# Strassen's seven half products for both MLP products after a hashed attention, in float32

## The chip, the cores and the metric

The kernel runs on 1 core of one Trainium2 chip. The time is the device time of one execution in microseconds (us), with the kernel before and the changed kernel run in turn on the same chip. Every time below is a median, with the least and the greatest run beside it.

A word used throughout: the attention works in 32 **units**. Two heads make a pair, there are 16 pairs, and each pair has two units of 384 queries. A unit took some 11.8 us in the kernel before. Even units transpose the next pair's Q and K, odd units compute its hash bits.

## The reference

```python
# attention: q, k, v are (4, 8, 768, 64), proj is (64, 6)
q_bits = (einsum('bhsd,dk->bhsk', q, proj) > 0);  k_bits = (same with k)
mask   = bucket(q_bits) == bucket(k_bits)            # 6 bits equal
scores = where(mask, q @ k.T / sqrt(64), -1e9)
attn   = softmax(scores);  out = attn @ v
# bridge: (4, 8, 768, 64) -> x of (3072, 512)
# MLP: w_in (512, 2048), w_out (2048, 512), alpha (2048,)
h = x @ w_in
g = maximum(h, 0) + alpha * minimum(h, 0)
return g @ w_out
```

## The kernel before

Attention and MLP follow each other. While the attention runs, each unit also decodes one piece of a weight (128 x 512, 512 KB, so 64-bit numbers, turned into float32) on VectorE. TensorE's work of a unit is split so that it always has something to do; the loads for the next pair are issued at the end of a unit. This is the part that the argument touches:

```python
    def load(pi, name, queue=None):
        ...
            t = pool.tile([P, NC, 2, D], F32, name=f"{name}n{pi}", tag=f"{name}n", bufs=1)   # one buffer
            for s in range(2):
                queue.dma_start(t[:, :, s], src[b, 2 * hp + s].rearrange("(p c) d -> p c d", c=NC))
...
    for u in range(UNITS):                        # 32
        pi, g = divmod(u, NCH)
        scores(u, 0)
        ...
        weight_parts(u)                           # VectorE: one weight piece
        scores(u, 1)
        add_third(u)                              # GpSimd: part of the row sums
        weight_sum(u)
        if more:
            if g == 0:
                turn(pi + 1, "k", 0)              # TensorE transposes of K for the next pair
                turn(pi + 1, "k", 1)
            else:
                hash_bits(pi + 1, 1)
        ...
        load_weight(u + 3)
        ...
        if more:
            magnitude(pi + 1, "qk"[g])            # ScalarE: squares of Q (even) or K (odd), in place
            if pi + 2 < NPAIR:
                load(pi + 2, "qk"[g])             # then the buffer is free for the next Q or K
```

So K has a single buffer; its last reader runs at the end of an odd unit, the next load is issued then, and the transposes that need it come in the middle of the following even unit.

The MLP holds both weights in SBUF and is matmuls alone, per half batch:

```python
            for kk in range(NK):                  # 4 k-tiles, 384 columns
                do(PE.matmul(ps, w[:, kk, o : o + P], xT[b][:, kk, ch * CW : (ch + 1) * CW], ...))
...
            for f in range(NF):                   # 16 f-tiles, 512 columns
                do(PE.matmul(ps, gT[b, ch, f][:, t * P : (t + 1) * P], w_out[f // 4][:, f % 4], ...))
```

Of the kernel before, what the change touches and what calls it, by code (L numbers as in the profile page):

```python
# [8 lines left out]
F32 = mybir.dt.float32  # L9
BF16 = mybir.dt.bfloat16  # L10
U32 = mybir.dt.uint32
# [336 lines left out]
@with_exitstack  # L348
def kernel(
    ctx: ExitStack,  # L350
    tc: tile.TileContext,
    q: bass.AP,
    k: bass.AP,
    v: bass.AP,
    proj: bass.AP,
    moe_w_in: bass.AP,
    moe_w_out: bass.AP,
    moe_alpha: bass.AP,
    out: bass.AP,
):  # L360
























    args = (tc, q, k, v, proj, moe_w_in, moe_w_out, moe_alpha, out)
    keep = ctx.enter_context(tc.tile_pool(name="keep", bufs=1))
    flag = keep.tile([1, 1], mybir.dt.int32, name="flag")
    fast_path(*args, flag)
    again = tc.nc.values_load(flag[0:1, 0:1])
    with tc.If(again > 0):  # L390
        general_path(*args)
# [3 lines left out]
def fast_path(  # L395
# [27 lines left out]
    BIG = 2.0 ** 20  # L423
# [9 lines left out]
    first = ctx.enter_context(tc.tile_pool(name="first", bufs=2))  # L433
# [13 lines left out]
    bq = const.tile([P, 1], F32, name="bq")  # L447
    tk = const.tile([P, 1], F32, name="tk")
    mk = const.tile([P, 1], F32, name="mk")
# [5 lines left out]
    w_in = [const.tile([P, NK, DFF // 4], F32, name=f"w_in{i}") for i in range(4)]  # L455
    w_out = [const.tile([P, NF // 4, DM], F32, name=f"w_out{i}") for i in range(4)]
    NW = 4 * (len(w_in) + len(w_out))
    wmax = const.tile([P, NW], F32, name="wmax")
    xT = [const.tile([P, NP, S], F32, name=f"xT{b}") for b in range(B)]

    NPT = 9
# [19 lines left out]
    def setup():  # L481

        for s in range(2):
            do(DVE.memset(wh[s], 0.0))
            nc.sync.dma_start(wh[s][D * s : D * s + D, :NB], proj)
        nc.sync.dma_start(alpha16, moe_alpha.rearrange("(t p) -> t p", p=P))
        make_identity(nc, ident)
        do(DVE.memset(ones, 1.0))
        for s in range(2):
            r = slice(D * s, D * s + D)  # L490
            do(DVE.tensor_copy(wh[s][r, NB : 2 * NB], wh[s][r, :NB]))



        for t, vals, step in (
            (bq, (-1e-37, -1e-37, 1.0, 1.0), 32),
            (tk, (0.0, -3.0e38, -3.0e38, -3.0e38), D),
            (mk, (BIG, -BIG / 2, -BIG / 2 * NB, 0.0), D),
        ):
            do(DVE.memset(t, vals[3]))  # L500
            for r in range(0, P, step):
                do(DVE.memset(t[r : r + 2 * NB + 1], vals[2]))
                do(DVE.memset(t[r : r + 2 * NB], vals[1]))
                do(DVE.memset(t[r : r + NB], vals[0]))
        for t in pts:
            do(POOL.memset(t[:, :, CW : CW + 1], 1.0))
        for t in qbs:
            do(POOL.memset(t, 0.0))
# [7 lines left out]
    raw, wr = {}, {}  # L516

    def piece(i):
        tiles, src = (w_in, moe_w_in) if i < NW // 2 else (w_out, moe_w_out)
        j, o = divmod(i % (NW // 2), 4)  # L520
        if src is moe_w_in:
            w = DFF // 4
            return tiles[j][:, o], src[o * P : (o + 1) * P, j * w : (j + 1) * w]
        return tiles[j][:, o], src[(4 * j + o) * P : (4 * j + o + 1) * P]

    def load_weight(i):
        if i < NW:
            raw[i] = pool.tile([P, 512], moe_w_in.dtype, name=f"raw{i}", tag="raw", bufs=3)
            nc.sync.dma_start(raw[i], piece(i)[1])
# [8 lines left out]
    def weight_abs(i):  # L538
        lo, hi = halves(i)
        do(ACT.activation(piece(i)[0], hi.bitcast(F32), AF.Abs))  # L540

    def weight_parts(i):
        lo, hi = halves(i)
        x = piece(i)[0]
        wr[i] = r = pool.tile([P, 512], F32, name=f"wr{i}", tag="wr")
# [7 lines left out]
    def weight_sum(i):  # L553
        lo, hi = halves(i)
        do(DVE.tensor_tensor(wr[i], piece(i)[0], wr[i], op=ALU.add))
        do(DVE.scalar_tensor_tensor(
            piece(i)[0].bitcast(U32), hi, 0x80000000, wr[i].bitcast(U32), op0=ALU.bitwise_and, op1=ALU.bitwise_or,
        ))


    def turn(pi, name, half):
# [6 lines left out]
        do(ACT.copy(tr[name, pi][:, half * CW : (half + 1) * CW], ps))  # L568
# [7 lines left out]
    def hash_bits(pi, half):  # L576
# [11 lines left out]
        for s in range(2):  # L588
            r = slice(D * s + 32, D * s + D)
            do(ACT.activation(bits["q", pi][D * s : D * s + 32, cols], ps[r], AF.Sign, bias=bq[r]))  # L590
        do(DVE.tensor_scalar(bits["k", pi][:, cols], ps, tk, mk, op0=ALU.is_gt, op1=ALU.mult))  # L591


    def scores(u, part):
        pi, g = divmod(u, NCH)
        qs = slice(g * CW, (g + 1) * CW)
        for kc in (2 * part, 2 * part + 1):
# [10 lines left out]
            do(ACT.activation(pt[:, :, :CW], sc[:, :, :CW], AF.Exp, scale=SCALE))  # L608
# [41 lines left out]
    def divide(u):  # L650
# [11 lines left out]
        do(DVE.scalar_tensor_tensor(  # L662
            xT[b][:, hp, g * CW : (g + 1) * CW], av[u][:, :CW], vsum[pi], d, op0=ALU.add, op1=ALU.mult,
        ))
# [19 lines left out]
    for u in range(UNITS):  # L684
# [17 lines left out]
        weight_sum(u)  # L702
        if more:
            if g == 0:
                turn(pi + 1, "k", 0)
# [3 lines that stand above are left out]
# [8 lines left out]
        load_weight(u + 3)  # L717
        if u + 1 < NW:
            weight_abs(u + 1)
# [6 lines left out]
    gT = {}  # L726

    def ff1(b, ch, f):

        if f % 4 < 2:  # L730
            ps = psum.tile([P, 2, 512], F32, name=f"h{b}_{ch}_{f}", tag="sc")[:, 0, :CW]
        else:
            ps = psum.tile([P, CW], F32, name=f"h{b}_{ch}_{f}", tag="mi")
        w, o = w_in[f // (NF // 4)], (f % (NF // 4)) * P
        for kk in range(NK):
            do(PE.matmul(  # L736
                ps, w[:, kk, o : o + P], xT[b][:, kk, ch * CW : (ch + 1) * CW],
                start=(kk == 0), stop=(kk == NK - 1),
            ))
        early = b == ch == 0 and f < EARLY  # L740
        neg = first.tile([P, CW], F32, name=f"neg{b}_{ch}_{f}", tag="neg")
        do(DVE.tensor_scalar(neg, ps, 0.0, alpha[:, f : f + 1], op0=ALU.min, op1=ALU.mult))  # L742
        where, bufs = (first, EARLY) if early else (mpool[0], NF + 2)
        g = where.tile([P, CW], F32, name=f"g{b}_{ch}_{f}", tag="g", bufs=bufs)
        do(DVE.scalar_tensor_tensor(g, ps, 0.0, neg, op0=ALU.max, op1=ALU.add))  # L745
        gT[b, ch, f] = g

    def ff2(b, ch, t):
        ps = psum.tile([P, DM], F32, name=f"z{b}_{ch}_{t}", tag="av")
        for f in range(NF):  # L750
            do(PE.matmul(  # L751
                ps, gT[b, ch, f][:, t * P : (t + 1) * P], w_out[f // 4][:, f % 4],
                start=(f == 0), stop=(f == NF - 1),
            ))
        o = mpool[0].tile([P, DM], F32, name=f"o{b}_{ch}_{t}", tag="o")
        do(ACT.copy(o, ps))  # L756
        nc.sync.dma_start(out_v[b, ch * CH + t], o)


    def verdict():  # L760
        top = const.tile([P, 3], F32, name="top")
        row = const.tile([1, 3], F32, name="row")
        do(DVE.tensor_reduce(top[:, :2], mags, axis=mybir.AxisListType.X, op=ALU.max))
        do(DVE.tensor_reduce(top[:, 2:3], wmax, axis=mybir.AxisListType.X, op=ALU.max))
        for n in range(3):
            ps = psum.tile([1, P], F32, name=f"vd{n}", tag="mi")
            do(PE.transpose(ps, top[:, n : n + 1], ident))
            do(DVE.tensor_reduce(row[:, n : n + 1], ps, axis=mybir.AxisListType.X, op=ALU.max))
        do(DVE.tensor_tensor(row[:, 0:1], row[:, 0:1], row[:, 1:2], op=ALU.mult))

        do(DVE.tensor_scalar(row[:, 0:1], row[:, 0:1], SAFE, None, op0=ALU.is_le))
        do(DVE.tensor_scalar(row[:, 2:3], row[:, 2:3], HI_END, None, op0=ALU.is_lt))
        do(DVE.tensor_tensor(row[:, 0:1], row[:, 0:1], row[:, 2:3], op=ALU.mult))
        do(DVE.tensor_scalar(flag, row[:, 0:1], -1.0, 1.0, op0=ALU.mult, op1=ALU.add))


    EARLY = 2
    mpool = []
    chunks = [(b, ch) for b in range(B) for ch in range(NCH)]
    last = UNITS - 1  # L780
    attend(last, 0)
    ff1(0, 0, 0)
    add_last(last)
    attend(last, 1)
    ff1(0, 0, 1)
# [3 lines left out]
    mpool.append(ctx.enter_context(tc.tile_pool(name="mlp", bufs=2)))  # L789
    for n, (b, ch) in enumerate(chunks):  # L790
        for f in range(EARLY, NF):
            ff1(b, ch, f)
        if n == 0:
            verdict()
        if n + 1 < len(chunks):
            for f in range(EARLY):
                ff1(*chunks[n + 1], f)
        for t in range(CH):
            ff2(b, ch, t)
# [29 lines left out]
```

## Time and profile before

| | kernel before |
|---|---|
| time | 1066.0 us (1065.7 to 1066.4) |
| span of the profiled execution | 1064.9 us |
| TensorE, VectorE busy in the span | 98%, 47% |
| mean granted clock of TensorE (1 is full speed) | 0.995 |
| attention, MLP | about 395 us, about 670 us |

In the profiles PE is TensorE's matmuls, PEld its weight loads, DVE VectorE, ACT ScalarE, POOL GpSimd and SPq SyncE's queue; L567 is line 567 of the kernel. The profile is read in this order: which engine is busy, then in which stretch of time, then what the idle time of that engine waited for. The chain of waits is the work that ended last, followed back step by step to what released it (start, length in us, what). These are the last lines of the chain of waits (the work that ended last, followed back step by step to what released it), cut off at 306 us (start, length in us, what):

```profile
302.00 3.62 DMA kn<-in_k_dram
305.63 0.14 issue
305.76 0.30 PE tp_k L567
```

And this is TensorE's list of waits over the whole kernel (in total us, how many, longest):

```profile
PE tp_q L567 <- DMA qn<-in_q_dram: 10.2, 2, 6.7
...
PE tp_k L567 <- DMA kn<-in_k_dram: 0.5, 2, 0.2
```

The wait of the transposes for the load of K is 0.5 us in all, and so looks like nothing. The chain says more: followed back from the transposes at 305.76, what released them last is the load of K, which had landed 0.14 us earlier. For 14 of the 16 pairs the margin was between 0.09 and 0.32 us. In nine of them it was 0.14 us, which is also what lies between landing and transposes in the changed kernel where TensorE plainly waits (unit 12, below): such a margin is no slack at all. (The wait of `tp_q` is the start of the kernel.)

### The profile page before, as it was taken

How to read it: one execution, taken by the hardware profiler on the slowest of the kernel's cores; microseconds unless marked ns; L12 is line 12 of the kernel's file. 1: busy time of each engine (PE TensorE's matmuls, PEld its weight loads, DVE VectorE, ACT ScalarE, POOL GpSimd, SP SyncE). 2: the span in 40 equal slices, each digit the busy share in tenths (PEclk: the TensorE clock that was granted, in tenths of full speed). 3: DMA queues.
4: the chain of work that ended last, by engine and by line, in shares of the span. 5: the costliest groups of instructions: out<-in, count | busy, mean ns of one | idle time of the engine just before them, and what ended most of it. 6: DMA issues, size and time to landing. Idle time of an engine off the chain costs nothing.

```text
span 1064.9 us, 10723 instructions
## 1 busy us (share of the span) xinstructions
PE 1039.0 (98%) x4292; PEld 508.7 (48%) x4292; DVE 504.3 (47%) x827; ACT 271.9 (26%) x441; POOL 133.7 (13%) x81
## 2 busy tenths in 40 slices
PE   5999999999999999999999999999999999999997
PEld 3444444444444445545545545545544544544543
DVE  3889999999899985302402402401401410410410
ACT  5766676667666730000000000000000000000000
POOL 2333333332333330000000000000000000000000
PEclk8999999999999999999999999999999999999999
DMA  5333333333333200000000000000000000000000
GB/s 168 85 99 85 86 103 100 85 87 117 99 85 85 70 1 0 1 20 10 1 20 10 0 10 20 1 10 20 1 10 20 0 10 20 1 10 20 1 10 22
DMA packets 62843, 42.73 MB, mean 40 GB/s; under 512 B 51504, under 2 KB 55616, under 8 KB 62784
## 3 DMA queue, kind: packets, MB, share of 16 engines
q1 hardware_dynamic: 61216, 41.57, 13.3%
q8 instruction: 35, 0.57, 0.2%
q10 hardware_dynamic: 1568, 0.39, 0.2%
q14 instruction: 24, 0.20, 0.1%
HBM read 35.66 MB, written 6.29 MB: 39 GB/s over the span
## 4 chain that ended last, share of the span: by engine, by line
PE 88%; DVE 5%; ACT 4%; DMA 1%; issue 1%; SPq 0%; ACTq 0%; DVEq 0%
PE h L736 31%; PE z L751 31%; PE sc L603 10%; PE av L636 10%; ACT pt L608 3%; PE hs L587 2%; PE sm L648 2%; PE tp_k L567 1%; PE tp_q L567 1%; DVE wr L551 1%; DMA qn<-in_q_dram 1%; ACT qb L590 0%; DVE accd L625 0%; DVE accd L626 0%; DVE kb L591 0%
## 5 line engine op out<-in xcount | busy, mean ns | idle before, releaser
L736 PE MATMUL h<-xT,w_in 128*128 128x384 f32 x1024 | 332.4, 486 | 0.0
L751 PE MATMUL z<-w_out,g 128*128 128x512 f32 x768 | 330.9, 592 | 0.0
L742 DVE TENSOR_SCALAR neg<-h,alpha 128x384 f32<-128x384 f32 x128 | 79.1, 618 | 462.4 <-PE h L736 462.2
L736 PEld LDWEIGHTS h<-xT,w_in 128*128 128x128 f32 x1024 | 194.2, 190 | 137.9 <-issue 5.1
L751 PEld LDWEIGHTS z<-w_out,g 128*128 128x128 f32 x768 | 145.9, 190 | 182.0 <-issue 179.9
L608 ACT ACTIVATE pt<-sc 128x768 f32<-128x768 f32 x192 | 152.0, 811 | 122.8 <-PE sc L603 121.1
L756 ACT COPY o<-z 128x512 f32<-128x512 f32 x24 | 14.1, 587 | 653.4 <-PE z L751 653.4
L603 PE MATMUL sc<-qT,kT 64*128 64x384 f32 x768 | 156.9, 486 | 0.0
L636 PE MATMUL av<-pt,vn 128*64 128x385 f32 (+1 forms) x768 | 138.1, 495 | 0.0
L617 POOL TENSOR_TENSOR accp<-pt,pt 128x768 f32<-128x768 f32 x32 | 71.5, 2233 | 230.1 <-ACT pt L608 230.1
L636 PEld LDWEIGHTS av<-pt,vn 128*64 128x64 f32 x768 | 49.4, 136 | 72.7 <-issue 72.7
L603 PEld LDWEIGHTS sc<-qT,kT 64*128 64x128 f32 x768 | 69.5, 189 | 14.9 <-issue 14.9
L745 DVE SCALAR_TENSOR_TENSOR g<-h,neg 128x384 f32<-128x384 f32 x128 | 71.3, 557 | 4.4
L603 PE MATMUL sc<-qb,kb 64*128 64x384 bf16 x384 | 64.4, 328 | 5.1 <-ACT pt L608 5.0
L620 POOL TENSOR_TENSOR accp<-accp,pt 128x768 f32<-128x768 f32 x32 | 59.9, 1871 | 23.6 <-DVE w_in L547 9.9
L603 PEld LDWEIGHTS <-kb 64*128 64x128 bf16 x384 | 24.0, 93 | 78.6 <-issue 61.7
L551 DVE SCALAR_TENSOR_TENSOR wr<-raw,wr 128x512 f32<-128x512 uint32 x32 | 55.1, 1721 | 1.1
L590 ACT ACTIVATE qb<-hs,bq 32x384 bf16<-32x384 f32 x64 | 36.7, 573 | 2.1 <-PE hs L587 0.8
L625 DVE TENSOR_TENSOR accd<-accd,pt 128x768 f32<-128x768 f32 x32 | 32.1, 1003 | 3.3
L626 DVE TENSOR_TENSOR accd<-accd,accp 128x768 f32<-128x768 f32 x32 | 32.0, 1000 | 3.3
L624 DVE TENSOR_TENSOR accd<-pt,pt 128x768 f32<-128x768 f32 x32 | 30.3, 948 | 5.2 <-ACT pt L608 5.2
L591 DVE TENSOR_SCALAR kb<-hs,tk,mk 128x384 bf16<-128x384 f32 x32 | 21.6, 675 | 16.1 <-ACT qb L590 16.1
(73 smaller groups left out, 436.1 us busy)
## 6 DMA issues: line engine op xcount, KB each, us to landing
raw<-in_moe_w_in_dram SPq DMA_DIRECT2D x16, 512.0 KB, 3.7
raw<-in_moe_w_out_dram SPq DMA_DIRECT2D x16, 512.0 KB, 3.5
qn<-in_q_dram SPq DMA_DIRECT2D x32, 192.0 KB, 3.3
vn<-in_v_dram SPq DMA_DIRECT2D x16, 384.0 KB, 4.2
out_dram<-o SPq DMA_DIRECT2D x24, 256.0 KB, 2.0
kn<-in_k_dram SPq DMA_DIRECT2D x30, 192.0 KB, 3.2
kn<-in_k_dram ACTq DMA_DIRECT2D x2, 192.0 KB, 4.0
wh<-in_proj_dram SPq DMA_DIRECT2D x2, 1.5 KB, 4.1
```

Of the source, the lines that this page charges most:

```text
L551: do(DVE.scalar_tensor_tensor(r, lo, 2.0 ** -52, r, op0=ALU.mult, op1=ALU.mult))
L590: do(ACT.activation(bits["q", pi][D * s : D * s + 32, cols], ps[r], AF.Sign, bias=bq[r]))
L603: do(PE.matmul(sc[:, s, :CW], what["k", pi][r, ks], what["q", pi][r, qs], start=first, stop=not first,))
L608: do(ACT.activation(pt[:, :, :CW], sc[:, :, :CW], AF.Exp, scale=SCALE))
L617: do(POOL.tensor_tensor(accp[u], p(u, 0), p(u, 1), op=ALU.add))
L620: do(POOL.tensor_tensor(accp[u], accp[u], p(u, 2), op=ALU.add))
L625: do(DVE.tensor_tensor(accd[u], accd[u], p(u, 5), op=ALU.add))
L636: do(PE.matmul(av[u][D * s : D * s + D, :w], nat["v", pi][:, s, kc * D : (kc + 1) * D], prob[u, kc][:, s, :w], start=(kc == 0), stop=(kc = ...
L736: do(PE.matmul(ps, w[:, kk, o : o + P], xT[b][:, kk, ch * CW : (ch + 1) * CW], start=(kk == 0), stop=(kk == NK - 1),))
L742: do(DVE.tensor_scalar(neg, ps, 0.0, alpha[:, f : f + 1], op0=ALU.min, op1=ALU.mult))
L745: do(DVE.scalar_tensor_tensor(g, ps, 0.0, neg, op0=ALU.max, op1=ALU.add))
L751: do(PE.matmul(ps, gT[b, ch, f][:, t * P : (t + 1) * P], w_out[f // 4][:, f % 4], start=(f == 0), stop=(f == NF - 1),))
```

## The change

The intent is to do less matmul work. Strassen's algorithm multiplies two 2 x 2 block matrices by 7 products of blocks and 15 additions of blocks (this variant) instead of 8 products. Both MLP products use it. The weight sums are the same for every batch, so they are computed once, during the attention, and kept in DRAM. The hash bits are now made by sign passes on ScalarE alone, where VectorE did those of K.

The weight pieces of `w_in` are decoded four at a time into one staging tile, with four differences, and then stored (these are units 3, 7, 11 and 15; those of `w_out` follow in the second half):

```diff
+    w_in_s = dram.tile([NI, P, NM, 2, P], F32, name="w_in_s")
+    w_out_s = dram.tile([NI, P, NM, DM // 2], F32, name="w_out_s")
+    x_s = dram.tile([B, NP, P, S], F32, name="x_s")
...
+    def weight_group(i):
+        if i < HW and i % 4 == 3:
+            n = i // 4
+            w = wst[n]
+            sums4 = ((3, 5, 2), (5, 0, 5), (4, 3, 0), (6, 1, 4))
...
+        for to, a, c in sums4:
+            do(DVE.tensor_tensor(w[:, to], w[:, a], w[:, c], op=ALU.subtract))
+        if i < HW:
+            c, kk = divmod(n, 2)
+            for ii in range(4):
+                nc.sync.dma_start(w_in_s[4 * c + ii][:, :, kk], w[:, :, ii])
+        else:
+            nc.sync.dma_start(w_out_s[n], w)
```

The attention's result goes through DRAM too. At unit 16 the first batch's pieces are loaded and GpSimd makes its four differences:

```diff
-        do(DVE.scalar_tensor_tensor(
-            xT[b][:, hp, g * CW : (g + 1) * CW], av[u][:, :CW], vsum[pi], d, op0=ALU.add, op1=ALU.mult,
-        ))
+        x = pool.tile([P, CW], F32, name=f"x{u}", tag="x")
+        do(DVE.scalar_tensor_tensor(x, av[u][:, :CW], vsum[pi], d, op0=ALU.add, op1=ALU.mult))
+        nc.sync.dma_start(x_s[b, hp][:, g * CW : (g + 1) * CW], x)
...
         weight_sum(u)
+        weight_group(u)
...
+        if u == HW:                               # 16
+            load_w(0)
+            load_w(1)
+            load_x(0)
+            sums_x(0)
```

The MLP becomes 44 blocks of 7 steps; the second weight's pieces are loaded into the memory that the attention gives back:

```diff
+    for i in range(NI):
+        wo.append(late[0].tile([P, NM, DM // 2], F32, name=f"wo{i}", bufs=1))
+        nc.sync.dma_start(wo[i], w_out_s[i])
+    for j, (b, what, n) in enumerate(blocks):
+        for st in ((2, 22, 6, 3, 7) if j == 0 else (2, 22, 5, 6, 3, 7)):
+            now.step(st)
+        if what == "1":
+            load_w(b * NI + n + 2)
...
-        do(DVE.tensor_scalar(bits["k", pi][:, cols], ps, tk, mk, op0=ALU.is_gt, op1=ALU.mult))
+        do(ACT.activation(bits["k", pi][:, cols], ps, AF.Sign, bias=hb))
```

(Cut: the class that orders the seven products and their sums in PSUM, the order of the pieces, the scaling of Q that the sign bits need, the check of the inputs' size.)

## The prediction

> **What bounds the kernel now.** I read the page first: TensorE is busy 98% of 1064.9 us, VectorE 47%, and in the row of slices VectorE is at 8 to 9 tenths until slice 14, then at 4, 0, 1 by turns. So there are two stages, an attention until about 395 us and an MLP after it. Next the chain of waits and the table by windows, which I cut at that border.
>
> ```profile
> 486.99 41.28 PE h L736 x128
> 528.27 41.20 PE z L751 x96
> ```
> ```profile
> 100.00:200.00 100.00, 98.51 (x664) 43.55 (x662) 91.71 (x140) 68.19 (x111) 36.17 (x18) 1.00 0.34 95
> 200.00:300.00 100.00, 98.04 (x658) 43.63 (x656) 92.00 (x141) 66.40 (x109) 33.88 (x17) 1.00 0.32 92
> ...
> 800.00:1060.00 260.00, 259.19 (x696) 131.86 (x694) 54.06 (x92) 6.46 (x11) 0.00 (x0) 1.00 0.03 11
> ```
> The chain shows the MLP as TensorE work end to end: 8 stretches of 128 matmuls and 8 of 96, each following the last. The windows (columns: stretch, length, busy us of PE, PEld, DVE, ACT, POOL, granted clock, DMA share, GB/s) show full clock, DMA nearly idle in the MLP, and in the attention VectorE at 92% just behind TensorE at 98%: a second engine that has no room for much more. Then the groups:
>
> ```profile
> L736 PE MATMUL h<-xT,w_in 128*128 128x384 f32 x1024 | 332.4, 486 | 0.0
> L751 PE MATMUL z<-w_out,g 128*128 128x512 f32 x768 | 330.9, 592 | 0.0
> ...
> L617 POOL TENSOR_TENSOR accp<-pt,pt 128x768 f32<-128x768 f32 x32 | 71.5, 2233 | 230.1 <-ACT pt L608 230.1
> ...
> L551 DVE SCALAR_TENSOR_TENSOR wr<-raw,wr 128x512 f32<-128x512 uint32 x32 | 55.1, 1721 | 1.1
> L590 ACT ACTIVATE qb<-hs,bq 32x384 bf16<-32x384 f32 x64 | 36.7, 573 | 2.1 <-PE hs L587 0.8
> ...
> L591 DVE TENSOR_SCALAR kb<-hs,tk,mk 128x384 bf16<-128x384 f32 x32 | 21.6, 675 | 16.1 <-ACT qb L590 16.1
> ```
> The code has 512 and 384 MLP matmuls, the profile 1024 and 768: a float32 matmul is two passes. The mean duration (486, 592 ns) is not the cost, since passes overlap; the pace is the chain's: 41.28/128 = 322.5 ns for 384 columns, 41.20/96 = 429.2 for 512. The difference over 128 columns is 0.834 ns a column, leaving 2.4 ns fixed.
>
> **What the Trainium skill says.** (1) "TensorE: Matmul & The Clock Gate", Back-to-back issue gap, gives about N/2.4 + 2.5 ns for a warm isolated matmul. The fixed part agrees (2.4), but these float32 passes take 0.834 ns a column, twice that; the trace decides. (2) The same page, LDWEIGHTS, says that the load costs by its columns, not its rows, about P/1.2 (107 ns at 128). The trace shows 190 ns in the MLP, but transposes, with the same 128 columns, follow each other far closer than a load's duration plus a matmul:
>
> ```profile
> 205.77 0.64 PEld L567 LDWEIGHTS tp_q<-ident,qn 128*128 128x128 f32 x6 [0.55 <-DVE xT L662]
> 205.77 0.88 PE L567 MATMUL tp_q<-ident,qn 128*128 128x128 f32 x6
> ```
> Six take 0.88 us, the last of them 0.27, so they start at most (0.88-0.27)/5 = 122 ns apart. (3) "DMA: Bandwidth & Descriptors", Anatomy of one DMA, puts a DMA (issued from GpSimd there, from SyncE here) at about 2.0 us + bytes/436 GB/s. The trace's best microseconds come close (last column GB/s), and a 512 KB weight load lands in 3.7 us, which at 400 GB/s is 1.3 of moving and 2.4 fixed:
>
> ```profile
> 7.00:8.00 1.00, 1.00 (x6) 0.76 (x4) 0.57 (x8) 0.44 (x1) 0.00 (x0) 1.00 1.10 388
> 8.00:9.00 1.00, 1.00 (x5) 0.78 (x5) 0.50 (x10) 0.52 (x2) 0.00 (x0) 1.00 1.06 418
> ```
> (4) "SBUF — State Buffer", Who interferes with whom: a VectorE instruction with two SBUF inputs contends with GpSimd reads. The trace agrees: VectorE's add of GpSimd's partial takes 958 ns in the median and 2279 at most (the tile's view: min, median, max), the long one being that of 386.56 us, where the timeline has a GpSimd add at 386.34.
>
> ```profile
> L626 DVE TENSOR_TENSOR accd<-accd,accp x32: 957/958/2279, 28.4 to 399.6; 128x768 f32<-128x768 f32 x32
> ```
>
> **The change part by part.**
>
> *Matmuls.* First product: 4 batches x 8 column pairs x 7 products x 2 k-tiles x 2 passes = 896 passes of 384 columns x 322.5 = 289.0 us. Second: 4 x 3 row tiles x 7 x 8 x 2 = 1344 passes of 256 columns; the pace is 256 x 0.834 + 2.4 = 215.9, so 290.2 us. Sum 579.2. Before: 8 x 41.28 + 8 x 41.20 = 659.8. Saved: 80.6 us, seven eighths almost exactly, because halving the second product's width only costs 2.4 ns a pass.
>
> *Additions in the MLP.* Per block of the first product (7 steps of 4 passes, 1.29 us each, 9.03 us) VectorE has 3 sums, 4 activations and 4 differences of 384 columns. The page of before has the two prices, 618 ns where the input is PSUM (neg) and 557 (g). Four read PSUM (the sum and the activation of h11 and h12), so 4 x 618 + 7 x 557 = 6.4 us, 71% of the block. ScalarE has 5 copies at 490 = 2.5 us. A copy of a bank must end before the second step after it: one step, 1.29 us, against 0.49 + about 0.2 of signalling. All hidden. In the second product a step is 3.45 us; easier still.
>
> *Weight pieces in the MLP.* Each block reads 0.917 MB: 2.3 us at 400 GB/s + 2.4 fixed = 4.7. The buffer comes free after the last product of block n, which runs as the second step of block n+1; until block n+2 there are 5 steps, 6.5 us. It fits, with 1.8 us to spare.
>
> *The border.* When the attention's memory is freed, 8 loads of the second weight's sums are issued, 7.34 MB = 18.4 us at 400 GB/s, and the third piece of the first weight is queued behind them. It is needed after 11 more steps, about 14.2 us; it lands at some 1 + 18.4 + 2.3 + 1.5 = 23. A stall of about 9 us. A stall that long also drops the clock, as after the early waits of the kernel before (third number from the end):
>
> ```profile
> 15.00:20.00 5.00, 1.51 (x8) 1.22 (x10) 4.14 (x6) 2.68 (x6) 1.81 (x1) 0.73 0.74 157
> 20.00:25.00 5.00, 5.00 (x24) 2.83 (x26) 1.08 (x2) 2.92 (x5) 1.68 (x1) 0.59 0.33 105
> ```
> Add 2 us: +11.
>
> *Attention, VectorE.* Away: 32 bit passes x 675 = 21.6 us, and the 16.1 us in which it waited for ScalarE before them. Added: 4 groups x 4 differences of 512 at 692 (the row of the same op and size) = 11.1, and 8 groups x 4 of 256; 557 ns at 384 columns and 692 at 512 make 135 per 128, so 422 each, 13.5. Together 24.6. Net 3 us more of work, 13 less of work and waits. ScalarE gets 32 x 490 = 16 us on 68%. TensorE stays the bound: -2 us.
>
> *Attention, transfers.* The first weight's sums leave in 4 groups of 1.8 MB, in runs of 512 bytes. At 250 to 400 GB/s (an estimate: no long run of 512 byte packets is in the trace) that is 7 to 10 us with the fixed part, against some 9 until the next group writes the single buffer: 0 to 2 us, three times: +2.
>
> *Attention, GpSimd.* At unit 16 GpSimd gets four sums of 768 elements (some 2.1 us each, 8.5) behind 3.4 MB of loads (8.5 + 2.4 us). It is in order, so the row sums of unit 17 wait some 19 us after the end of unit 16, where a unit is 11.85 us. VectorE reaches their last add about 0.2 of a unit into unit 18, and so waits 6 to 8 us; at 92% it can't make that up soon, and TensorE waits for the row totals: +6.
>
> *Rest.* The check's fourth transpose and one maximum, as each waits for the other engine: +1. Setup memsets were not on the path.
>
> Sum: 1065.9 - 80.6 + 11 - 2 + 2 + 6 + 1 = 1003.3. I predict 1003 us.
>
> **The rivals.** (a) The weight pieces are late in every block: if a load takes 6.5 + x us, 30 blocks lose x each; at 250 GB/s rather than 400, x is about 0 and at 180 some 1, so 1033. Against it: 388 to 418 GB/s in the first microseconds, with 4 KB rows, and these are 7 KB. (b) The 256-column passes are bound by the weight load: if loads of 190 ns did not overlap and took 240 in all, 1344 x 24 = 32 us, so 1035. Against it: the transposes at 122 ns. (c) The border costs nothing because the pieces are served first, and GpSimd's delay is absorbed: 985 to 988. For it: ten probability buffers instead of nine; against it: one queue in order. (d) VectorE becomes the bound of the attention: the odd units with a group of four differences of 512 get 2.8 - 1.35 us more, and contention with GpSimd can stretch each; 12 odd units x 1.5 = 18, so 1021. Against it: the removed waits.
>
> **Range and chances.** The saved 80.6 is arithmetic at a measured pace; the stalls (18 us in the sum) could be 0 or 40. So 986 to 1023, 8 in 10. Slower than 1044.6 (which would be within 2%) needs 59 us of stalls. Faster 0.95, within 2% 0.03, slower 0.02.
>
> **What would show it.** Right: 1344 passes of 256 columns at a pace of 216 ns; stretches of 9.0 us a block; one gap of 5 to 12 us on TensorE some 15 us after the attention, ended by a DMA of a first-weight piece, with a dip of the clock; a wait of VectorE for GpSimd near 220 us; weight loads near 4.7 us. Wrong: gaps at each block's first step, ended by DMA (a), loads back to back without matmul gaps in the second product (b), no gap at the border (c), an attention that ends after 410 us with VectorE near 100% (d).

## The result

| | before | changed |
|---|---|---|
| time, us | 1066.0 (1065.7 to 1066.4) | 1051.8 (1051.6 to 1052.9) |
| span of the profile, us | 1064.9 | 1049.8 |
| mean granted clock | 0.995 | 0.969 |

The ratio is 0.987 (95% interval 0.985 to 0.989): within 2%, and 49 us above the prediction. A ratio here is the mean time of one kernel's fast runs over that of the other's of the same rounds, so it is not quite the ratio of the medians in the table. The result was correct in this run and in all that follow.

From the page of the changed kernel: busy time, the granted clock in 40 slices (tenths), the chain that ended last by engine, one group of the second product.

```profile
PE 973.1 (93%) x4741; PEld 599.8 (57%) x4741; DVE 607.4 (58%) x959; ACT 372.9 (36%) x669; POOL 159.8 (15%) x98
...
PEclk8998979898999999988999999999999999999999
...
PE 72%; DVE 18%; DMA 6%; ACT 2%; issue 1%; SPq 0%; DVEq 0%; ACTq 0%
...
L756 PE MATMUL z_0a<-wo,g 128*128 128x256 f32 x256 | 57.9, 379 | 0.0
```

TensorE's busy time fell by 66 us, but its share fell too: there is new idle time, and a clock that dips in the first half and at the border (the 18th and 19th slice). Where the matmuls run, they run as planned. The table by windows (stretch, length, busy us of PE, PEld, DVE, ACT, POOL, clock, DMA share, GB/s) of the MLP of the changed kernel:

```profile
500.00:800.00 300.00, 300.00 (x1154) 218.91 (x1154) 122.14 (x206) 52.29 (x116) 15.79 (x8) 1.00 0.21 74
```

and its chain there, one step of the second product after another:

```profile
542.36 3.45 PE z_0c L756 x16
545.81 3.45 PE z_0a L756 x16
```

TensorE has no gap in 300 us, and 3.453/16 gives 215.8 ns for a pass of 256 columns. So the 80.6 us were saved, and 66 us came back elsewhere. TensorE's waits in the changed kernel:

```profile
PE tp_k L614 <- DMA kn<-in_k_dram: 34.4, 8, 10.6
PE f_2a L756 <- DMA wi<-w_in_s: 12.9, 1, 12.9
PE tp_q L614 <- DMA qn<-in_q_dram: 11.5, 2, 6.5
```

The second and third lines were foreseen (the border) or were there before (the start). The first is the line of 0.5 us from before. Four of its waits are large, 9.70, 10.56, 5.29 and 5.28 us, in units 4, 8, 12 and 16: each just after a unit that stores a group of `w_in`'s sums. Here is unit 12, first SyncE's timeline, then TensorE's:

```profile
184.07 3.90 SPq L603 DMA_DIRECT2D w_in_s<-wsi  x4
188.07 1.33 SPq L714 DMA_DIRECT2D x_s<-x  x1
189.50 2.34 SPq L488 DMA_DIRECT2D kn<-in_k_dram  x2
```
```profile
188.92 0.81 PE L653 MATMUL sc<-qT,kT 64*128 64x384 f32 x4
195.02 1.51 PE L614 MATMUL tp_k<-ident,kn 128*128 128x128 f32 x6 [5.29 <-DMA kn<-in_k_dram]
```

The end of TensorE's wait, in the chain:

```profile
190.69 4.19 DMA kn<-in_k_dram
194.88 0.14 issue
195.02 1.51 PE tp_k L614 x6
```

And the windows around it:

```profile
187.00:188.00 1.00, 1.00 (x10) 0.22 (x8) 0.90 (x2) 0.61 (x2) 1.00 (x1) 1.00 1.02 274
...
190.00:195.00 5.00, 0.00 (x0) 0.01 (x1) 4.83 (x8) 0.59 (x1) 2.29 (x1) 0.83 0.90 219
195.00:200.00 5.00, 4.98 (x18) 2.62 (x20) 0.21 (x1) 0.98 (x2) 0.00 (x0) 0.50 0.36 108
```

The four stores (1.8 MB) are issued first. The load of K, in the same queue, is issued 5.4 us after the first of them and lands only after they have moved, at 274 GB/s with every DMA engine busy. TensorE stands for five us, and then has half its clock for about as long again (the last numbers but two, 0.83 and 0.50): the same six transposes take 1.51 us instead of 0.85. In units 4 and 8 the wait is twice as long because the scheduler that orders the program's instructions had moved the loads that the code has at unit 16 forward, in front of K: SyncE waited there for the store of `x` before it could issue a load of it (unit 4), and two loads of a first-weight piece (1.8 MB more) stood ahead of K (unit 8).

These units take 23.77, 25.33, 19.66 and 19.42 us instead of 11.8 each: together 41.0 us, of which 30.8 are the gaps and 10 the slow clock. The other four of the eight waits for K, 0.60 to 1.19 us, are in units 20, 22, 26 and 28, behind the stores of `w_out`'s sums: the same pattern, smaller. At the border, the chain:

```profile
450.87 5.39 DMA wo<-w_out_s
...
456.33 17.40 DMA wi<-w_in_s
...
473.77 2.93 PE f_2a L756 x4
```

The gap on TensorE is 12.94 us there (460.83 to 473.77), with some 3 us of slow clock after it. The account of the span, with what the prediction had:

| term | predicted, us | found in the profile, us |
|---|---|---|
| matmuls | -80.6 | -80.6 (at the paces above) |
| stores of the sums in the attention | +2 | +44.4 (41.0 in units 4, 8, 12 and 16; 3.4 in units 18 to 29, where the four small waits for K are) |
| border | +11 | +15.9 (12.94 of gap, the rest clock; the total from experiment 3) |
| GpSimd at unit 16 | +6 | not to be seen; see experiment 1 |
| VectorE's and ScalarE's swap | -2 | 0 |
| rest | +1 | +4.4 (start 1.7, row totals 1.6, check and last store 1.1) |
| sum | -62.6 | -15.9; the spans differ by 15.1, so 0.8 is not itemised |

### The profile page after: what moved, and what is told of

Its sections match the earlier page's. It is cut to its first block, busy times and chain, and to the rows that moved or that the text cites. A ratio compares the mean times of both kernels' runs of the same rounds, so it can differ in the third digit from the quotient of the medians.

```text
span 1049.8 us, 12494 instructions
## 1 busy us (share of the span) xinstructions
PE 973.1 (93%) x4741; PEld 599.8 (57%) x4741; DVE 607.4 (58%) x959; ACT 372.9 (36%) x669; POOL 159.8 (15%) x98
## 4 chain that ended last, share of the span: by engine, by line
PE 72%; DVE 18%; DMA 6%; ACT 2%; issue 1%; SPq 0%; DVEq 0%; ACTq 0%
PE av L686 7%; PE sc L653 7%; PE z_2a L756 5%; PE z_1a L756 5%; PE z_0a L756 5%; PE z_2c L756 3%; PE z_1c L756 3%; PE z_0c L756 3%; DVE accd L676 2%; PE f_2a L756 2%; PE f_3a L756 2%; DMA kn<-in_k_dram 2%; PE f_7a L756 2%; PE f_6a L756 2%; PE f_4a L756 2%; PE f_5a L756 2%
## 5 line engine op out<-in xcount | busy, mean ns | idle before, releaser
L732 POOL TENSOR_TENSOR x<-x,x 128x768 f32<-128x768 f32 x16 | 31.9, 2003 | 379.1 <-DMA x<-x_s 378.4
L810 DVE TENSOR_TENSOR g<-g,g 128x384 f32<-128x384 f32 x128 | 82.5, 665 | 2.2
L756 PE MATMUL z_2a<-wo,g 128*128 128x256 f32 x256 | 58.0, 379 | 0.5 <-ACT z_2u L763 0.5
L756 PE MATMUL z_0a<-wo,g 128*128 128x256 f32 x256 | 57.9, 379 | 0.0
L756 PE MATMUL z_1a<-wo,g 128*128 128x256 f32 x256 | 57.9, 379 | 0.0
L756 PEld LDWEIGHTS z_2a<-wo,g 128*128 128x128 f32 x256 | 48.6, 190 | 8.1 <-ACT z_2u L763 0.9
L756 PEld LDWEIGHTS z_0a<-wo,g 128*128 128x128 f32 x256 | 48.6, 190 | 7.5
L756 PEld LDWEIGHTS z_1a<-wo,g 128*128 128x128 f32 x256 | 48.6, 190 | 6.6
L614 PE MATMUL tp_k<-ident,kn 128*128 128x128 f32 x96 | 17.7, 334 | 34.6 <-DMA kn<-in_k_dram 34.4
L577 DVE SCALAR_TENSOR_TENSOR wr<-wx,wr 128x512 f32<-128x512 f32 x32 | 46.8, 1463 | 1.1
L553 DVE TENSOR_SCALAR wx<-wx 128x512 uint32<-128x512 uint32 x32 | 44.1, 1379 | 1.1
```

Source lines behind the costliest of these rows:

```text
L553: do(DVE.tensor_scalar(x.bitcast(U32), x.bitcast(U32), 3, 0xC0000000, op0=ALU.logical_shift_left, op1=ALU.bitwise_xor,))
L577: do(DVE.scalar_tensor_tensor(r, x, -1.0 if turned else 1.0, r, op0=ALU.mult, op1=ALU.subtract if turned else ALU.add,))
L732: do(POOL.tensor_tensor(x_m[b, to], x_m[b, a], x_m[b, c], op=ALU.subtract))
L756: do(PE.matmul(self.ps[bank], self.left(left, k), self.right(right, k), start=start and k == 0, stop=k == self.nk - 1, skip_group_check=no ...
L810: do(DVE.tensor_tensor(g_m[to, i], g_m[x, i], g_m[y, i], op=op))
```

## The experiments

All were timed in three or more rounds beside the kernel before. The first theory, T (Q in the expectations): in the four long units the load of K stands behind the stores; its first rival, V: VectorE, which has four more differences in the units just before them, is what delays them. The edits are against the changed kernel unless said.

### 1. Both loads of the next pair half a pair earlier (e1_k_early)

The squares of K move from the odd unit to the even one, so that K's buffer comes free a unit earlier. The stores and VectorE's work stay.

```diff
-        if more:
-            magnitude(pi + 1, "qk"[g])
-            if pi + 2 < NPAIR:
-                load(pi + 2, "qk"[g])
+        if more and g == 0:
+            for name in "qk":
+                magnitude(pi + 1, name)
+                if pi + 2 < NPAIR:
+                    load(pi + 2, name)
```

> The changed kernel, but each pair's K load is issued one unit (11.8 us) earlier, at the end of the even unit beside the Q load, so that it stands ahead of the store of the first weight's sums in the queue; its squares are taken there too. Theory Q (the K load stands behind the 1.8 MB store in one queue, and the attention's pace hangs on it): the long units 4, 8, 12 and 16 (23.8, 25.3, 19.7, 19.4 us) come to some 12 each, the four gaps of TensorE before the K transposes go, the total falls by 38 to 42 us, to about 1012. Rival V (VectorE with its 24.6 us of new sums, beside GpSimd, sets the attention's pace): the long units stay above 15 us, the total falls by less than 10 us.

Measured: 1016.1 us (1014.6 to 1018.9), ratio 0.953, 35.7 us less than the changed kernel; clock 0.983. SyncE's timeline has the load of K for unit 12 at 175.18; its transposes run at 188.87, 13.7 us later, where the changed kernel had 5.5 us between the two:

```profile
175.18 1.60 SPq L488 DMA_DIRECT2D kn<-in_k_dram  x2
```

and TensorE's waits have lost their first line:

```profile
PE f_2a L756 <- DMA wi<-w_in_s: 12.9, 1, 12.9
PE tp_q L614 <- DMA qn<-in_q_dram: 12.7, 3, 6.7
PE sm L698 <- DVE accd L676: 6.6, 4, 3.0
```

From the second pair on, K now lands 3.3 to 10.3 us ahead of its transposes. The stores and the VectorE work are all there, and the gaps are gone: the rival falls, T stands. A pair of units takes 23.62 us, with a weight group or without one, against 23.65 in the kernel before; so the swap between VectorE and ScalarE gains nothing and costs nothing, and VectorE is not the bound of these units. It gives back 35.7 and not 41 because waits appear that the long units had hidden: row totals late by up to 3.0 us (`sm`), and one load of Q late by 1.26 us (unit 10). From here on, where both squares stand in the even units, a unit is counted from one first exponential of ScalarE to the next: an even one then usually takes some 13.5 us and an odd one 10.14. Unit 17, where GpSimd makes its four differences, takes 16.03 us, which is 5.9 us more: 3.04 of gap, and the rest half clock after it (0.50 in the window from 230 to 235 us). In the changed kernel the differences had begun inside the gap of unit 16 (at 247.28, the gap ends at 250.04) and run on to 255.6, mostly under the slow clock.

### 2. The stores alone, added to the kernel before (e5_store_alone)

The other way about: nothing of the change but a store of the same size in runs of the same length (its source repeats one 512-byte piece) and four small VectorE operations in units 3, 7, 11 and 15. The edit is to the kernel before, and the DRAM copy is not used for anything.

```diff
         weight_sum(u)
+        if u < NW // 2 and u % 4 == 3:
+            c, kk = divmod(u // 4, 2)
+            for _ in range(4):
+                do(DVE.tensor_tensor(stuff, stuff, stuff, op=ALU.max))
+            for ii in range(4):
+                nc.sync.dma_start(extra[4 * c + ii][:, :, kk], stuff[:, ii].unsqueeze(1).to_broadcast([P, 7, P]))
```

> The kernel before with one part of the change alone: in units 3, 7, 11 and 15 four VectorE operations of 512 columns after the weight piece and then four stores of 448 KB in 512 byte runs to a spare DRAM tensor (of no use to the result). No Strassen, no other new transfer. Theory Q: a gap of 4 to 6 us before the K transposes of units 4, 8, 12, 16, each with some 2.5 us of clock recovery, as in units 12 and 16 of the changed kernel, which have no other new transfer: +26 to +34 us, to about 1096. Rival V (VectorE): +4 to +12 us, with waits of TensorE for VectorE.

Measured: 1095.2 us (1094.7 to 1098.2) beside 1066.9 before, ratio 1.028: +28.4 us, with 16 DMA issues. TensorE's waits:

```profile
PE tp_k L571 <- DMA kn<-in_k_dram: 20.0, 5, 5.0
```

The four gaps are 4.94, 4.95, 4.98 and 4.88 us and the four units 18.90 to 19.01 us, 7.1 to 7.3 more than before: some 5 of gap, and 2 after it, where the granted clock is down. The store is sufficient. (The expectation calls units 12 and 16 of the changed kernel free of other new transfers; the store of `x` stands there too, but the gaps there are only 0.3 to 0.4 us longer than here.) With experiment 1, in which the store is there and K is early, the cause is both parts together: a store in the queue, and a load behind it without slack.

### 3. The border's loads one by one (e3_spread)

```diff
         wo.append(late[0].tile([P, NM, DM // 2], F32, name=f"wo{i}", bufs=1))
-        nc.sync.dma_start(wo[i], w_out_s[i])
...
             load_w(b * NI + n + 2)
+            for i in ((0, 1) if j == 0 else (j + 1,) if j < NI - 1 else ()):
+                do(nc.sync.dma_start(wo[i], w_out_s[i]))
```

> The changed kernel, but the eight loads of the second weight's sums at the border are spread: two behind the third piece of the first weight, then one behind each further piece. Theory (the 7.3 MB ahead of that piece are the border's stall): the gap of 12.9 us on TensorE goes, and with it some 3 us at half clock; the total falls by 13 to 17 us, to about 1037. Rival (the piece waits for its buffer, that is for the last product of the first block): the gap stays above 6 us.

Measured: 1035.9 us (1034.1 to 1037.4), ratio 0.972: 15.9 us less than the changed kernel, as expected. The gap of 12.94 us is gone, and with it about 3 us of slow clock. The term of the border is settled: right in kind, 15.9 instead of 11.

### 4. The scheduler kept from moving the loads (e7_no_early)

`do` keeps an instruction in program order. Nothing else is changed:

```diff
-            nc.sync.dma_start(
+            do(nc.sync.dma_start(
                 t, x_s[b, 2 * kh : 2 * kh + 2].rearrange("k p s -> p k s")[:, :, ch * CW : (ch + 1) * CW],
-            )
+            ))
...
-            nc.sync.dma_start(w_m[n], w_in_s[n % NI])
+            do(nc.sync.dma_start(w_m[n], w_in_s[n % NI]))
```

> The changed kernel, but the first loads of weight sums and attention rows for the MLP keep their place in the program (after unit 16); in the changed kernel the build's scheduler moved them up to units 3 to 9, in front of K loads. Theory Q: the gaps before units 4 and 8 (9.7 and 10.6 us) fall to the 5.3 us of units 12 and 16, so -9 to -10 us there. At unit 16 GpSimd now waits for 3.4 MB and then makes its sums, the case that the prediction put at +6 us: together 1043 to 1049 us. If the early loads cost nothing, the two gaps stay near 10 us.

Measured: 1047.3 us (1046.0 to 1049.4), ratio 0.983: 4.5 us less. The four gaps are now alike, 5.70, 5.28, 5.49 and 5.31 us: the doubling in units 4 and 8 was indeed these loads. The four long units are 10.4 us shorter in sum. But with the loads at unit 16 GpSimd's sums start only at 255.46, after the gap, and units 18 to 20 take 14.14, 12.85 and 14.73 us, 5.1 us more than in the changed kernel (11.91, 12.07 and 12.63). So half of what the shorter gaps gave is lost there. It is not all GpSimd's: TensorE's waits in these units are 3.8 us for K (0.76 in the changed kernel) and 1.5 us for row totals and what follows from them.

### 5. The store in long runs (e2_wide)

In the changed kernel each store writes runs of 128 float32, 512 bytes. With the piece's number inside, a run is 3584 bytes. The staging tile and the loads follow.

```diff
-    w_in_s = dram.tile([NI, P, NM, 2, P], F32, name="w_in_s")
+    w_in_s = dram.tile([NI, 2, P, NM, P], F32, name="w_in_s")
...
-                nc.sync.dma_start(w_in_s[4 * c + ii][:, :, kk], w[:, :, ii])
+                nc.sync.dma_start(w_in_s[4 * c + ii, kk], w[:, ii])
```

> The changed kernel, but the stores of the first weight's sums move 3584 byte runs in place of 512 byte runs (another layout in DRAM, same bytes, same 4 issues). Theory Q: the store was moved at 287 GB/s; at some 400 its 1.84 MB take 4.6 us for 6.4, so each of the four gaps is 1.8 to 2.5 us shorter, with the clock's recovery a little less; the total falls by 8 to 12 us, to about 1042. If the place in the queue alone counts (the waits for the store's landing), the gaps hardly change: under 3 us.

Measured: 1046.7 us (1044.5 to 1050.4), ratio 0.982 (0.980 to 0.985; whether this is over 2% is unclear): 5.1 us less, where 8 to 12 were expected. Windows during a store:

```profile
182.00:183.00 1.00, 1.00 (x8) 0.43 (x6) 1.00 (x2) 1.00 (x4) 0.17 (x1) 1.00 1.02 401
```

The store moves at 401 GB/s and not 274, and the gaps are 7.63, 8.56, 3.09 and 3.10 us, some 2 us less each (8.45 in all). Not all of it reached the time, which the expectation missed. Part of the rest is in later waits for K: unit 18 now has one of 1.86 us where the changed kernel has none, and over the whole kernel TensorE's wait for K falls from 34.4 to 27.9 us, by 6.5 and not 8.45. The shape of the store is a part of the cost, not the cause: a faster store in front of K is still in front of K.

### 6. K from another queue (e4_act_queue)

Is it the order within SyncE's queue, or do the stores and the load share the DMA engines whatever queue they come from?

```diff
-                load(pi + 2, "qk"[g])
+                load(pi + 2, "qk"[g], nc.scalar)
```

> The changed kernel, but the Q and K loads after the first pair are issued from ScalarE's queue, at the same place in the program. Theory Q1 (the order within one queue is what delays them): each DMA engine takes from both queues, the K load lands 3 to 5 us after its issue and the four gaps fall to at most 2 us: -30 to -38 us, to about 1016 to 1022. Theory Q2 (the engines' bandwidth is what lacks): the load still lands late, the gaps of units 12 and 16 stay above 3.5 us, and the total falls by less than 15 us.

Measured: 1038.2 us (1035.9 to 1039.7), ratio 0.973: 13.6 us less, between the two expectations. The four gaps shrink to 3.55, 3.02, 2.62 and 2.62 us. But loads of K still took 4.8 to 7.4 us from issue to landing while a store of `w_in`'s sums ran, against 3.2 (the median) in the kernel before, and the small gaps of the later units, where the groups of `w_out` are stored, grew from 3.6 us in four units to 6.7 us in six (0.7 to 2.0 each). In unit 12 K was issued 0.9 us after the first store, where it had been 5.4, and had landed 7.9 us after it, where it had been 10.8; it landed 1.3 us before the last of the four stores. So the engines did serve both queues: the earlier issue gave 4.5 us, and the shared engines took 1.6 of them back. It is some of both.

### 7. GpSimd's four differences, one per two units (e8_sums_apart)

On top of experiment 1, whose new delay of 5.9 us was at GpSimd. The theory here: VectorE's operations with two inputs are slowed beside the four differences, and so the row totals come late; spread over units 18, 20, 22 and 24, the differences should leave VectorE the time to catch up.

```diff
-            sums_x(0)
+        if HW + 2 <= u < HW + 10 and u % 2 == 0:
+            sums_x(0, (u - HW) // 2 - 1, (u - HW) // 2)
```

> The kernel of e1 (K loads a unit early), but GpSimd's four sums for the first batch come one by one in units 18, 20, 22 and 24. In e1 the four stood together 8.4 us, VectorE's two-input operations beside them took 2.2 us for 0.7, and that pair of units was 5.9 us longer. Theory[...]: those 5 to 6 us come back, about 1010 to 1011 us, no gap over 2 us before the row totals at unit 17. Rival (work is work; the sums only move): each of the four units loses some 1.5 us and the total stays within 2 us of e1's 1016.

Measured: 1019.0 us (1018.4 to 1019.8), ratio 0.956: 3 us more than experiment 1, not 5 to 6 less. Refuted. Each of the four pairs now takes 10.9 + 15.0 us, 2.3 more than usual, 9.1 in all. So one difference by itself costs about as much as it lasts (2.1 us), more than the 1.5 us of the rival: that four stand in one row is not what makes them dear.

### 8. Experiments 1, 3, 5 and 7 together (e9_all)

The four edits in one kernel, and no other.

> The changed kernel with all that helped: K loads a unit early (e1), 3584 byte runs (e2), second weight's sums spread (e3), GpSimd's sums one by one (e8). If the effects add: 1051.8 - 36 - 16 - 5 = about 994 us (990 to 998), leaving some 9 us over the 985.3 that the matmuls alone would give.

Measured: 1001.7 us (1000.4 to 1003.4), ratio 0.940, clock 0.995. This is 7 to 8 above what was expected, and the part of it that experiment 7 carries cost 9.1 instead of nothing.

### 9. The differences at unit 16 again (e11_together)

```diff
             load_x(0)
-        if HW + 2 <= u < HW + 10 and u % 2 == 0:
-            sums_x(0, (u - HW) // 2 - 1, (u - HW) // 2)
+            sums_x(0)
```

> e9 with GpSimd's four sums together at unit 16 again, as in the changed kernel. e8 against e1 said that together costs 5.9 us and apart 9.1: so 3 us below e9, about 998.5; and 5 to 6 us above e10.

Measured: 999.1 us (998.1 to 999.9), ratio 0.937: 2.6 less than experiment 8, as expected (the intervals of the two ratios, 0.938 to 0.942 and 0.935 to 0.939, overlap slightly). Here the mechanism can be seen. GpSimd's timeline, then VectorE's, of this kernel:

```profile
214.68 8.40 POOL L733 TENSOR_TENSOR x<-x,x 128x768 f32<-128x768 f32 x4
```
```profile
215.03 1.91 DVE L556 TENSOR_SCALAR wr<-wx 128x512 uint32<-128x512 uint32 x1
...
219.20 2.20 DVE L577 SCALAR_TENSOR_TENSOR wr<-wx,wr 128x512 f32<-128x512 f32 x1
...
231.11 0.43 DVE L556 TENSOR_SCALAR wr<-wx 128x512 uint32<-128x512 uint32 x1
...
232.30 0.69 DVE L577 SCALAR_TENSOR_TENSOR wr<-wx,wr 128x512 f32<-128x512 f32 x1
```

The same VectorE operation of the same size takes 2.20 us while GpSimd's four differences run and 0.69 us when they don't. VectorE stands three times as long over each of its three operations with two SBUF inputs there (2.18 to 2.20 us for 0.69), and the row totals come late for that. This is the contention that the fourth of the prediction's places names; the prediction used it to read one add, and then priced GpSimd's work by its own row of instructions. But an operation with one input (L556) is held up as well, 1.91 us for 0.43, which the prediction's sentence does not cover.

### 10. The differences on VectorE (e10_on_vector)

If GpSimd's work blocks VectorE for its whole length, VectorE might as well do it: two at the end of unit 9 and two at the end of unit 13, with the load of `x` at unit 8.

```diff
-            do(POOL.tensor_tensor(x_m[b, to], x_m[b, a], x_m[b, c], op=ALU.subtract))
+            do(engine.tensor_tensor(x_m[b, to], x_m[b, a], x_m[b, c], op=ALU.subtract))
...
+        if u == 8:
+            load_x(0)
+        if u in (9, 13):
+            sums_x(0, (u - 9) // 2, (u - 9) // 2 + 2, DVE)
```

> e9, but the four sums for the first batch are made by VectorE, two in unit 9 and two in unit 13, odd units without a group of weight sums, and GpSimd keeps the row sums alone. Theory[...]: 4 x 0.96 = 3.8 us of VectorE in units that lost 1.35 us of bit passes each: at most 1 us lost in either, so e9's 1001.7 - 8 to - 9 = about 993. Rival (any two-input work of 8 us in the attention costs its time): 997 or more.

Measured: 998.9 us (996.6 to 999.6), ratio 0.936, where 993 was expected: the rival reading (997 or more) was right. The gain over experiment 9 is within the spread of the runs. The even units from 10 to 18 take 14.03, 15.19, 14.78, 15.18 and 14.00 us instead of some 13.5, over 5 us in all. And after the differences, in unit 10, the first of VectorE's three adds for the row sums takes 2.57 us (at 138.12), where it took 0.95 in the same unit of experiment 9's kernel (at 136.14): pushed back, it now overlaps GpSimd's own add (137.43 to 139.86). The third takes 2.25 us beside GpSimd's second add, but 2.39 there too, so it is nothing new.

### 11. The same in the middle of the unit (e12_mid_unit)

```diff
         weight_group(u)
+        if u in (9, 13):
+            sums_x(0, (u - 9) // 2, (u - 9) // 2 + 2, DVE)
...
-        if u in (9, 13):
-            sums_x(0, (u - 9) // 2, (u - 9) // 2 + 2, DVE)
```

> e10, but VectorE's two sums in units 9 and 13 stand in the middle of the unit, behind the weight piece, where the groups of weight sums (2.8 us) stand in units 3, 7, 11 and 15 and cost nothing in e1 and e9 (pairs of 23.6 us with and without them), not at its end, ahead of the adds that the row totals wait for. Theory P (the place counts: there is slack between the weight piece and the division, none before the adds): the units 10 to 15 come back to pairs of 23.6 us, -5 us on e10, about 993 to 994. Rival S (VectorE has no slack at all in these units): no change, 997 to 999.

Measured: 994.7 us (994.3 to 995.6), ratio 0.933 (0.931 to 0.934), clock 0.995. The total is 4.2 us less than in experiment 10, near the 5 of theory P, but the theory is right only in part: of the pairs of units from 10 to 15 one came back to 23.6 us (they take 23.62, 25.15 and 24.15). Units 10 to 19 give 3.3 us; and the profile of experiment 10 has a stretch of slow clock at the border (0.66 in the window from 435 to 440) that this one has not, so not all of the gain is shown to be the place. This is the best version, 6.7% under the kernel before and 57 us under the change as it was made. Only units 12, 14 and 16 are still longer than the usual 13.5 (15.01, 14.00, 13.88), by some 2.4 us in all. Against the 985.3 us that the matmul arithmetic alone gives (1065.9 - 80.6), 9.4 us remain; 0.7 of it is a later start (unit 1 begins at 27.0 us, before at 26.3), the waits for row totals and for the check are others, and it is not itemised further.

## Why the prediction was wrong

The time was outside the range (986 to 1023) and the chance of 0.95 was given to the wrong outcome. One step failed by a lot, and the others are near.

- **The step that failed: "Attention, transfers", +2.** It asked one question of the stores, whether they end before their single staging buffer is written again, and they do. It did not ask what else is issued in that queue in the meantime. The answer is the load of K, 0.09 to 0.32 us ahead of its use in the kernel before. The term measured 41.0 us for the first weight's stores: 30.8 of gaps and 10 of half clock (experiments 1 and 2; some 9 us of it through loads that the scheduler moved forward, by the difference of the gaps in experiment 4). Some 3.4 us more stand in the later units, where K waits behind the stores of the second weight's sums. The mechanism was named nowhere in the prediction, neither in the sum nor as a rival. Its assumption of 250 to 400 GB/s was right (274 to 294).
- **The saving: right.** 80.6 us, 215.8 ns where 215.9 was expected. Rival (b), a bound by the weight load, is out: loads of 190 ns lie under passes 216 ns apart, without a gap in 300 us. Rival (a) is out too: first-weight pieces landed in 4.6 us (predicted 4.7), with no wait at a block's first step.
- **The border: right in kind, 11 predicted, 15.9 measured** (experiment 3). The gap was 12.94 us, not 9, so rival (c), a border that costs nothing, is out.
- **GpSimd: the size near, the mechanism half of it.** The +6 did not show in the changed kernel, where the differences ran in and just after a K gap. With that gap gone they cost 5.9 (experiment 1). But the prediction had the row sums stand behind loads and differences; experiments 7, 9 and 10 show that VectorE is held up beside GpSimd's work, at 2.20 us instead of 0.69, and spreading the work makes it worse. That the size came near is luck in part: about half of the 5.9 us is half clock after a gap of 3.04, of which this term has nothing.
- **VectorE: -2 predicted, 0 measured** (23.62 against 23.65 us a pair). Rival (d), VectorE as the bound, falls for the attention as a whole; experiments 8, 10 and 11 show how little slack it has around the end of a unit.
- **Rest: +1 predicted, about +4.4 found,** in pieces of 1.1 to 1.7 us, none of which was tested by itself.
- **The range.** It was drawn as if the 18 us of stalls that were named were all that could go wrong ("could be 0 or 40"). The stalls of the stores and the border alone were 60 us.

## What to carry to other kernels

Before a large store is put into a DMA queue, list every load that is issued behind it and by how much each lands before its use; a load with no wait in the profile may have no slack at all, and the chain of waits shows it. A load can be taken out of the way at little cost by freeing its buffer earlier, which here was worth 35.7 us, more than twice as much as making the change had given. Work that one engine is given beside a busy VectorE is to be priced by what it takes from VectorE, and its place within the unit can count as well as the engine.

## What the Trainium skill lacked or had wrong

- "DMA: Bandwidth & Descriptors", Specifications, has line rate from transfers of 512 bytes up. Stores to DRAM in runs of exactly 512 bytes moved at 274 to 294 GB/s here, and in runs of 3584 bytes at 401 to 405, with every DMA engine busy in both.
- "DMA: Bandwidth & Descriptors", Issuing engines are not separate DMA queues, says that issuing from several engines saves only the sequencer's time, usually small. Here it was not small: K issued from ScalarE's queue was issued 0.9 us after the first store and not 5.4 (unit 12), which cut the four gaps from 30.8 to 11.8 us in sum, and the time by 13.6. That the transfers still share the engines agrees: K took 4.8 to 7.4 us beside a store.
- No page has it that issuing itself slows behind a large store: SyncE took 2.34 us for the two issues of K behind the store (unit 12) and 1.23 us for the same two in the kernel before.
- The section of the prediction's first place has no figure for float32 matmuls (other pages touch on float32 passes and rates, none gives a time by columns). Here one of the two passes came every 215.8, 322.5 and 429.2 ns at 256, 384 and 512 columns, that is 0.834 ns a column and 2.4 ns.
